# A windowed decode attention with a gated unit: Wq loaded in three transfers of 2, 6 and 24 KB per partition instead of two of 8 and 24, and x in two pieces instead of three

## The chip, the cores and the metric

The kernel runs on one core of one Trainium2 chip. The metric is device time in microseconds (us), the median of several executions. The profile is one further execution of the same program, recorded instruction by instruction and DMA packet by DMA packet.

The engines have short names: PE is TensorE (PEld its weight loads), DVE is VectorE, ACT is ScalarE, POOL is GpSimd, and SP issues transfers. SPq and ACTq are the instruction streams of SP and ACT when they issue a DMA. A core has 16 DMA engines; they are called **lanes** here, since every large transfer of this kernel is cut into 128 rows (one for each SBUF partition), eight for each lane. In the records, the transfers that SP issues are queue q1, those that ACT issues q10, and instruction fetches q8.

## What is computed

```python
xn = _layernorm(x, axis=-1)              # x: 8 x 1 x 512, bf16
# A: attention over the last W = 2048 of 8192 cached keys, 32 query heads on 8 KV heads
q = (xn @ wq)                            # wq: 512 x 4096
scores = einsum("bhqd,bhkd->bhqk", q, k) * (Dh ** -0.5)
o = einsum("bhqk,bhkd->bhqd", softmax(scores), v)
s = o @ wo                               # wo: 4096 x 512
# B: gated unit
g = _silu((_sigmoid(xn @ w_gate) * (xn @ w_up)) @ w_down)     # F = 1792
return x + s * g
```

There are 8 batch rows of one token each. The window of the K cache is 32 MB and that of the V cache 32 MB in bf16; Wq and Wo are 4 MB each, and the three weights of the gated unit 1.75 MB each. Each byte is read once, 81.01 MB in all.

## The kernel before

The order of all instructions is written out by hand; no scheduler moves them.

**Transfers.** ACT issues x (lines 124 to 129) as its first instructions, in three pieces: columns 0 to 255, 256 to 383 and 384 to 511 of the 8 rows. All the large loads go through SP by the helper `load` (its `dma_start` is line 116). SP's first two are Wq: each partition's 32 KB of Wq are 4 rows of the contraction index kt, 8 KB each, and the first transfer brings row kt = 0 (`WQ0` = 4096 elements), the second the other three. Then the K tiles (line 142, 8 tiles of 4 MB), the V tiles (line 157, 16 of 2 MB), the weights of the gated unit, and Wo in six pieces (line 185). Wq, K, the gated unit's weights and Wo share a ring of three buffers (`KRING` = 3), V has a ring of four (`VRING` = 4). `issue_loads` (line 216) issues the next load of a fixed list as soon as its ring has a buffer that the program has released; SP then waits until the buffer's last readers are done. Wq, K tile 0 and K tile 1 fill the K ring, and so K tile 2 takes the buffer of Wq and has to wait for the q projection.

**The start.** DVE computes the layernorm of x from line 244 (it waits for all pieces of x) to line 257; PE transposes xn (267) and copies x itself into another layout (272); DVE writes `xnT_sb` (285). The q projection (`q_projection`, line 396) is 32 matmuls (line 405), in the order group gg, then kt, then head gl: each reads 512 columns of row kt of Wq. `q_out` (416) casts the result on ACT (419), transposes it on DVE (424) and spreads it into `qz_sb` by copies on DVE (434) and ACT (436). `q_out` of group 0 stands before the loop, that of group 1 (line 682) after the first two K transposes.

**The loop.** From line 669 each step t transposes one eighth of a K tile on DVE (`k_turn`, line 464), multiplies q with an eighth that was transposed four steps earlier (`qk`, line 479), and, 52 steps later, multiplies the probabilities with a quarter of a V tile (`pv`, line 609). The softmax parts stand at fixed steps. At the end come the gated unit, the sum over Wo (line 723), two operations on DVE (734, 736) and the store of the result (738).

Of the kernel before, what the change touches and what calls it, by code (L numbers as in the profile page):

```python
# [10 lines left out]
def kernel(  # L11
# [16 lines left out]
    _, Hkv, Sk, Dh = A_k_cache.shape  # L28
    Hq = A_wq.shape[1] // Dh
# [3 lines left out]
    KT = D // P  # L33
# [46 lines left out]
    NSUM = 4  # L80
    NCOL = 2
    DC = D // NCOL
    WQ0 = 4096

    bf16 = mybir.dt.bfloat16
    f32 = mybir.dt.float32
# [26 lines left out]
    def load(dst, src, q=None):  # L113
        if q is None:
            q = nc.sync
        q.dma_start(out=dst, in_=src)  # L116
# [5 lines left out]
        return vring.tile(shape, bf16, name=name, tag="vring", align_bytes=ALIGN)  # L122

    x_bf = work.tile([B, D], bf16, name="x_bf")
    for c0, c1 in ((0, 2), (2, 3), (3, 4)):
        nc.scalar.dma_start(
            out=x_bf[:, P * c0 : P * c1],
            in_=A_x.flatten_outer_dims()[:, P * c0 : P * c1],
        )

    wq_sb = k_tile([P, KT, Hq * Dh], "wq_sb")
    wq_rows = A_wq.rearrange("(p kt) n -> p (kt n)", kt=KT)
    wq_flat = wq_sb[:].rearrange("p kt n -> p (kt n)")
    load(wq_flat[:, :WQ0], wq_rows[:, :WQ0])
    load(wq_flat[:, WQ0:], wq_rows[:, WQ0:])

    k_tiles = {}
    v_tiles = {}
# [633 lines left out]
```

## Time and profile before

| | before |
|---|---|
| time, median of 3 executions | 197.48 us (197.15 to 197.74) |
| the profiled execution's own time | 197.29 us |
| its span, first to last instruction | 195.5 us |
| so, around the span | 1.8 us |
| moved by q1 (all of SP's loads) | 5056 packets, 81.01 MB |
| busy: PE / DVE / ACT / POOL | 53% / 54% / 16% / 2% of the span |

The page of the profile shows the share of time in which the lanes were moving packets, in 40 slices of 4.9 us, and the rate. The *timeline* lists instructions in order of time, each with the idle time of its engine before it and what ended it. The *windows* view gives the busy time of each engine, the share of the lanes' time and the rate in any stretch; packets are counted where they begin, so a share over a short stretch can exceed 1. The *chain* goes back from the last instruction to what released each step.

The trace also keeps each DMA packet with its start, duration, size and queue. At the start of the program these records read (start of the first packet of the group, end of the last, all lanes together):

| packets | size of each | one takes | from, to (us) |
|---|---|---|---|
| first piece of x, 8 | 512 B | 25 ns | 1.71 to 1.80 |
| first transfer of Wq, 128 | 8192 B | 309 ns (the first ones up to 1044) | 1.80 to 4.99 |
| second transfer of Wq, 128 | 24576 B | 912 ns | 4.78 to 12.30 |
| second piece of x, 8 | 256 B | 18 ns | 5.70 to 5.92 |
| third piece of x, 8 | 256 B | 18 ns | 7.54 to 7.76 |
| completion packets of the third piece, 8 | 4 B | 9 ns | 8.46 to 8.67 |
| first K tile | 32768 B | 1213 ns | from 12.05 |

A transfer ends with one completion packet of 4 bytes (9 ns) on each lane that carries it; these packets raise the semaphore for which the readers wait.

### The profile page before, as it was taken

What the parts mean: (1) busy time and instruction counts of PE and PEld (TensorE: products, weight loads), DVE (VectorE), ACT (ScalarE), POOL (GpSimd) and SP (SyncE); (2) the same over time, 40 slices, a digit from 0 to 9 for tenths busy, and PEclk for the clock granted to TensorE, in tenths of its full rate; (3) what the DMA queues carried; (4) which work ended last, traced back from release to release, by engine and by line L of the source; (5) the groups of instructions that cost most, each with busy time, mean ns of one, the idle gap of its engine ahead of it and who ended that gap; (6) DMA issues with size and microseconds to landing.
All of it is one profiled execution on the core that took longest, in us unless ns stands there. A gap on an engine that the chain in (4) does not pass through costs nothing.

```text
span 195.5 us, 1888 instructions
## 1 busy us (share of the span) xinstructions
PE 102.9 (53%) x750; PEld 36.2 (19%) x750; DVE 105.5 (54%) x149; ACT 30.8 (16%) x69; POOL 4.6 (2%) x25
## 2 busy tenths in 40 slices
PE   0062014434323258403695989858944893577763
PEld 0020001101000012100121222322311131223551
DVE  0156499999899998899969726403100010040301
ACT  2025050000000084000011143511111114010100
POOL 8000000000000000000000000000000000000000
PEclk9999999999999999955588799988999798597999
DMA  7999999999999999999999999999999999999990
GB/s 276 423 476 429 436 429 429 429 429 421 429 429 429 429 429 429 389 432 463 429 419 432 436 422 429 427 429 429 429 429 432 429 431 425 431 429 432 425 390 30
DMA packets 5128, 81.14 MB, mean 415 GB/s; under 512 B 616, under 2 KB 896, under 8 KB 1152
## 3 DMA queue, kind: packets, MB, share of 16 engines
q1 hardware_dynamic: 5056, 81.01, 97.0%
q8 instruction: 6, 0.10, 0.2%
q10 hardware_dynamic: 64, 0.01, 0.0%
q14 instruction: 2, 0.02, 0.0%
HBM read 81.01 MB, written 0.01 MB: 414 GB/s over the span
## 4 chain that ended last, share of the span: by engine, by line
DMA 62%; DVE 23%; PE 10%; issue 1%; ACT 1%; SPq 0%; DVEq 0%
DMA k_sb<-in_A_k_cache_dram 31%; DMA v_sb<-in_A_v_cache_dram 22%; DVE k_sb L464 18%; DMA wo_sb<-in_A_wo_dram 10%; PE acc_ps L609 4%; DVE pt_bf L527 2%; PE s_ps L479 2%; PE pT_ps L540 2%; PE o_ps L635 2%; DVE mx L493 1%; SPq L116 0%; DVE qz_sb L434 0%; DVE o_sb L644 0%; PE den_ps L584 0%; DVE qT_sb L424 0%
## 5 line engine op out<-in xcount | busy, mean ns | idle before, releaser
L464 DVE STREAM_TRANSPOSE k_sb<-k_sb 128x1024 f32<-128x1024 f32 x64 | 73.7, 1210 | 6.7 <-DMA k_sb<-in_A_k_cache_dram 6.6
L479 PE MATMUL s_ps<-k_sb,qz_sb 128*32 128x512 bf16 x256 | 29.8, 565 | 54.2 <-DVE k_sb L464 48.4
L609 PE MATMUL acc_ps<-v_sb,pT_sb 128*64 128x512 bf16 x256 | 39.6, 443 | 10.7 <-DMA v_sb<-in_A_v_cache_dram 10.6
L644 DVE TENSOR_TENSOR o_sb<-o_ps,rden 16x512 bf16<-16x512 f32 (+2 forms) x6 | 3.0, 504 | 47.5 <-PE o_ps L635 47.5
L479 PEld LDWEIGHTS <-qz_sb 128*32 128x32 bf16 x256 | 8.5, 116 | 78.6 <-issue 55.3
L623 ACT COPY acc_sb<-acc_ps 128x512 f32<-128x512 f32 x16 | 9.4, 586 | 84.7 <-PE acc_ps L609 84.7
L609 PEld LDWEIGHTS <-pT_sb 128*64 128x64 bf16 x256 | 13.3, 120 | 31.5 <-DMA v_sb<-in_A_v_cache_dram 14.6
L635 PE MATMUL o_ps<-acc_sb,Sel 128*16 128x512 f32 (+2 forms) x48 | 15.9, 477 | 3.4 <-ACT acc_sb L623 3.4
L561 DVE TENSOR_SCALAR pT_sb<-pc_bf,Hm 128x1024 bf16<-128x1024 bf16 x16 | 6.6, 477 | 6.7 <-PE acc_ps L609 6.7
L507 ACT ACT_TABLE_LOAD x1 | 1.3, 1283 | 39.9 <-DVE nm L501 39.9
L635 PEld LDWEIGHTS o_ps<-acc_sb,Sel 128*16 128x16 f32 x48 | 4.5, 103 | 14.9 <-issue 7.7
L493 DVE TENSOR_REDUCE mx<-s_ps 128x1 f32<-128x512 f32 x8 | 5.3, 662 | 3.2 <-PE s_ps L479 3.2
L540 PE MATMUL pT_ps<-pt_bf,spread 128*128 128x512 bf16 x16 | 6.0, 501 | 1.3 <-DVE pt_bf L527 0.7
L267 PE MATMUL xnT_ps<-ident,xn_bf 8*128 8x8 bf16 x4 | 0.3, 174 | 11.6 <-DVE xn_bf L257 11.6
L436 ACT COPY qz_sb<-qT_sb 32x32 bf16<-32x32 bf16 x20 | 4.8, 241 | 8.2 <-DVE qT_sb L424 7.9
L355 PE MATMUL d_ps<-wgu_sb,xnT_sb 128*32 128x448 bf16 x32 | 3.0, 511 | 5.3 <-DMA wgu_sb<-in_B_w_up_dram 3.0
L723 PE MATMUL a_ps<-wo_sb,o_sb 128*32 128x256 bf16 x64 | 4.5, 273 | 2.0 <-DMA wo_sb<-in_A_wo_dram 2.0
L507 ACT ACTIVATE p_bf<-s_ps,nm 128x512 bf16<-128x512 f32 x8 | 5.4, 686 | 0.0
L244 DVE CAST x_f<-x_bf 8x512 f32<-8x512 bf16 x1 | 0.4, 415 | 9.2 <-DMA x_bf<-in_A_x_dram 9.2
L548 ACT CAST pc_bf<-pT_ps 128x512 bf16<-128x512 f32 x8 | 4.5, 587 | 5.0 <-DVE pt_bf L527 2.8
L527 DVE STREAM_TRANSPOSE pt_bf<-p_bf 128x512 bf16<-128x512 bf16 x8 | 4.9, 668 | 0.0
L723 PEld LDWEIGHTS <-o_sb 128*32 128x32 bf16 x64 | 3.5, 96 | 3.1 <-issue 3.0
(59 smaller groups left out, 39.4 us busy)
## 6 DMA issues: line engine op xcount, KB each, us to landing
k_sb<-in_A_k_cache_dram SPq DMA_DIRECT2D x8, 4096.0 KB, 19.3
v_sb<-in_A_v_cache_dram SPq DMA_DIRECT2D x16, 2048.0 KB, 15.7
wq_sb<-in_A_wq_dram SPq DMA_DIRECT2D x1, 3072.0 KB, 11.4
wo_sb<-in_A_wo_dram SPq DMA_DIRECT2D x1, 2048.0 KB
wgu_sb<-in_B_w_gate_dram SPq DMA_DIRECT2D x1, 1792.0 KB
wgu_sb<-in_B_w_up_dram SPq DMA_DIRECT2D x1, 1792.0 KB, 24.7
wd_sb<-in_B_w_down_dram SPq DMA_DIRECT2D x1, 1792.0 KB
wq_sb<-in_A_wq_dram SPq DMA_DIRECT2D x1, 1024.0 KB, 4.6
```

Source lines behind the costliest of these rows:

```text
L436: nc.scalar.copy(out=out, in_=in_)
L464: nc.vector.transpose(out=kw, in_=kw)
L479: nc.tensor.matmul(s_tiles[i][32 * g : 32 * (g + 1), :], lhsT=qz_sb[:, hb, h, 2 * a + e, :], rhs=kT[:, :, a, h, :, e], start=(n == 0), sto ...
L493: nc.vector.reduce_max(out=mx_of[hb][:, kq : kq + 1], in_=s_tiles[i][:], axis=AX.X)
L507: nc.scalar.activation(out=p_bf[:, :, kq], in_=s_tiles.pop(NK * hb + kq)[:].rearrange("p (o c j) -> p c j o", o=2, j=NC), func=AF.Exp, bia ...
L527: nc.vector.transpose(out=pt[:, w * n : w * (n + 1)], in_=p_bf[:, w * n : w * (n + 1)])
L540: nc.tensor.matmul(pT_ps[:], lhsT=spread[:, gg, y].rearrange("p k g -> p (k g)"), rhs=pt[:, c, y, :], start=(y == 0), stop=(y == 1), skip_ ...
L561: nc.vector.tensor_scalar(out=pT_of[hb, gg][:, :, gl, :], in0=pc, scalar1=Hm[:, gl : gl + 1], scalar2=None, op0=ALU.mult,)
L609: nc.tensor.matmul(acc_tiles[i][w * c : w * (c + 1), :], lhsT=pT[:, GL * rep * ch : GL * rep * ch + w], rhs=v_tiles[i][:, ch : ch + NCH, : ...
L623: nc.scalar.copy(out=acc_sbs[i // NSUM][:, i % NSUM], in_=acc_tiles.pop(i)[:])
L635: nc.tensor.matmul(o_ps[rows, :n, :], lhsT=Sel[:, c].rearrange("p g r -> p (g r)"), rhs=acc_sb[:, :, Dh * c : Dh * (c + 1)], start=(c == 0 ...
L723: nc.tensor.matmul(a_ps[32 * c : 32 * (c + 1), :], lhsT=o2_sb[:, k, :], rhs=wo_parts[k][:, DC * c : DC * (c + 1)], start=(k == 0), stop=(k ...
```

## The change

The split of Wq becomes a list of bounds, in elements of each partition's 16384: 0, 1024, 4096, 16384. The first 8 KB, one transfer before, come in 2 KB and 6 KB; the last 24 KB stay one transfer. The second and third piece of x become one. SP issues one DMA more and ACT one less; the number of DMAs stays the same, and so do the semaphores that later transfers take in turn. In the order of instructions, PE's third matmul of the q projection (heads gl = 2, 3 of kt = 0) has a new wait, for the second transfer of Wq; the fifth (kt = 1) waits for the last transfer, as before. PE's copy of x waits for two pieces instead of three. Nothing else moves on any engine.

```diff
-    WQ0 = 4096
+    WQ_AT = (0, 1024, 4096, KT * Hq * Dh)
...
-    for c0, c1 in ((0, 2), (2, 3), (3, 4)):
+    for c0, c1 in ((0, 2), (2, 4)):
         nc.scalar.dma_start(
             out=x_bf[:, P * c0 : P * c1],
             in_=A_x.flatten_outer_dims()[:, P * c0 : P * c1],
...
-    load(wq_flat[:, :WQ0], wq_rows[:, :WQ0])
-    load(wq_flat[:, WQ0:], wq_rows[:, WQ0:])
+    for n0, n1 in zip(WQ_AT, WQ_AT[1:]):
+        load(wq_flat[:, n0:n1], wq_rows[:, n0:n1])
```

## The prediction

> **What bounds the kernel now.** I read the DMA rows of the page first. Here are the lanes' busy share in tenths and the rate, in 40 slices:
>
> ```profile
> DMA  7999999999999999999999999999999999999990
> GB/s 276 423 476 429 436 429 429 429 429 421 429 429 429 429 429 429 389 432 463 429 419 432 436 422 429 427 429 429 429 429 432 429 431 425 431 429 432 425 390 30
> ```
>
> Between the first and the last slice the lanes never rest. The windows view says it more finely (us; busy time of PE, PEld, DVE, ACT, POOL with counts; PE's clock; lanes' share; GB/s):
>
> ```profile
> 0.00:1.80 1.80, 0.00 (x0) 0.00 (x0) 0.00 (x0) 0.00 (x0) 1.20 (x7) 1.00 0.01 2
> 1.80:5.00 3.20, 0.00 (x0) 0.00 (x0) 0.00 (x0) 1.28 (x1) 3.03 (x17) 1.00 1.19 451
> 5.00:22.35 17.35, 4.24 (x38) 1.49 (x38) 6.28 (x24) 3.76 (x12) 0.36 (x3) 1.00 1.00 431
> 22.35:60.00 37.65, 13.28 (x112) 4.18 (x113) 36.83 (x38) 2.89 (x12) 0.00 (x0) 1.00 1.00 431
> ...
> 140.00:180.00 40.00, 24.98 (x166) 9.55 (x164) 2.99 (x5) 5.93 (x9) 0.00 (x0) 0.85 1.01 430
> 180.00:190.30 10.30, 7.48 (x94) 5.25 (x92) 1.99 (x3) 0.96 (x2) 0.00 (x0) 0.92 0.99 414
> 190.30:192.11 1.81, 1.59 (x22) 0.89 (x17) 0.00 (x0) 0.00 (x0) 0.00 (x0) 1.00 0.33 115
> 192.11:195.50 3.39, 0.29 (x2) 0.09 (x1) 0.70 (x2) 0.00 (x0) 0.00 (x0) 0.96 0.01 2
> ```
>
> From 1.80 to 190.3 us the share is 0.99 to 1.01 at 430 GB/s; DVE, nearly as full from 22 to 60 us (36.83 of 37.65), holds the lanes up nowhere. To see how close it comes, I set the bytes that SP had issued against the bytes moved, at each of SP's later issues: the least that was still queued is 2.56 MB, 6.2 us of work at 431 GB/s, at the K tile issued at 64.64 us. A load could be issued 6 us later and no lane would notice. So the time is a sum: start of the stream (1.80) + its length (to 192.11) + a tail of 3.40 (two matmuls, two DVE operations, the store) = 195.51, and 1.78 around the span makes 197.29, which is 0.19 below the median of the runs, 197.48.
>
> The timeline of the start shows why the work on x and q doesn't count (start, duration, what, [idle before <- what ended it]):
>
> ```profile
> 0.74 1.27 ACTq L126 DMA_DIRECT2D x_bf<-in_A_x_dram  x3
> ...
> 0.74 0.89 SPq L116 DMA_DIRECT2D wq_sb<-in_A_wq_dram  x2
> ...
> 9.15 0.41 DVE L244 CAST x_f<-x_bf 8x512 f32<-8x512 bf16 x1 [9.15 <-DMA x_bf<-in_A_x_dram]
> ...
> 12.19 3.69 PE L405 MATMUL q_ps<-wq_sb,xnT_sb 128*32 128x512 bf16 x32
> ...
> 17.89 0.48 DVE L652 MEMSET o_sb<- 128x512 uint32 x1
> 22.35 2.37 DVE L464 STREAM_TRANSPOSE k_sb<-k_sb 128x1024 f32<-128x1024 f32 x2 [3.98 <-DMA k_sb<-in_A_k_cache_dram]
> ```
>
> x lands at 9.15, the q projection ends at 15.88, DVE is through with everything it can do at 18.37, and then it sits 3.98 us until K tile 0 lands. The chain of waits agrees: it passes from SP's issues straight into the landing of that tile, by no instruction of x or q:
>
> ```profile
> 1.22 0.41 SPq L116
> 1.63 0.05 issue
> 1.68 20.65 DMA k_sb<-in_A_k_cache_dram
> ```
>
> **The change part by part.** *The split of Wq, as packets.* Each lane carried 8 packets of 8192 B at 309 ns. Now it carries 8 of 2048 B, which the pieces of Wo and others show at 84 ns, and 8 of 6144 B. That size is not in the trace; 4096 B take 159 ns and 8192 B 309, and the middle is 234. So 84 + 234 - 309 = 9 ns for each row, 8 rows: 72 ns, and one more completion packet, 9 ns. Sum: **+0.08 us** of stream on every lane.
>
> *x in two pieces.* The eight lanes that carry x spend 25 + 18 + 18 ns on data and three times 9 on completions now, and 2 x 25 + 2 x 9 afterwards: -0.02 us on those, nothing on the other eight. The stream ends with its slowest lane, so +0.06 to +0.08; I take **+0.07**.
>
> *The extra issue on SP.* One issue takes 0.41 to 0.64 us (Wq 0.42 and 0.41, K tile 0 0.64). K tiles 0 and 1 are issued some 0.46 us later, at 2.14 instead of 1.68; 4 MB are queued then, 9.7 us of work. Without that queue it would cost the 0.46.
>
> *The hand-over from the first to the second transfer* is the one place where the lanes could run dry. SP's first issue starts at 0.74 and its first packet at 1.80, 1.06 later. The second issue starts at 1.22, so its packets are there at 2.28. The first transfer keeps a lane busy for 8 x 84 = 0.67 us from 1.80, to 2.47 at the earliest. In truth it lasts longer, since the first packets are slow: over their row's 309 ns the first ones took up to 735 ns more, 0.41 us on average over the lanes. That leaves 0.2 to 0.6 us of margin: cost 0. From there the 6 KB packets last 1.87 us, and the third issue, at about 1.68, is there by 2.74.
>
> *The slow first packets themselves* are the term that the trace does not show for 2 KB. Bounds: if small first packets do away with that loss, -0.41; if they pay it twice, once for each size, +0.41. I take 0: it looks like the time to the first data, common to any size, and the nearest row is the same queue's own first packets.
>
> *x earlier.* The second piece of x is issued at 1.37, and 0.97 us after its issue the first piece was moving; so it was ready near 2.3, about when the second transfer of Wq was, and it came to its turn only behind eight 8 KB packets and one of 24 KB, at 5.70. Then data and completions of q10 alternated with single packets of 24 KB, 0.91 us each, until 8.67. With 2 KB packets ahead and 6 KB packets in between, the same order gives x at about 1.80 + 0.4 + 0.67 + 2 x 0.234 + the 0.5 that DVE starts after the last completion = 3.8; if all eight 6 KB packets and two of 24 KB go ahead first, 7.2. Either way 2 to 5 us before 9.15. DVE's part, PE's transposes and POOL's constants (done at 5.4) move ahead; but the q projection must wait at its fifth matmul for the last 24 KB of Wq. That landed 11.4 us after its issue at 1.22, at 12.6, and now 0.08 later. Its 28 matmuls at 0.107 follow: 15.7 instead of 15.88. So 5 us on x shrink to 0.2 on q, and these go into DVE's 3.98 us of waiting. The new wait on PE (third matmul, second transfer) has only q matmuls behind it; should q come late, DVE's 3.98 us and, for the issue of K tile 2 at 15.92, a queue of 15.9 us are in front of any harm.
>
> *ACT's missing issue*, 0.325 us, brings the table load forward to about 1.7; ACT then waits for DVE at 10.53 anyway: 0.
>
> *Tail.* Nothing there is touched: 0.
>
> **Sum:** 197.29 + 0.07 = 197.36 for a profiled execution; by the median, 197.48 + 0.07 = **197.55 us**. That is 0.04%, and a measurement of this kernel tells about 0.3% (0.6 us) from no change.
>
> **Rivals.** *Slower: a transfer pays its start each time.* If the second transfer began only when the first was through, as the first began 1.06 us after its issue, the lanes would stand idle for up to 1.06 us: 198.6. It decides as soon as packets of the second transfer reach the lanes after the first's have run out (2.5 to 2.9 us). Against it: the second transfer of Wq moves its first packet at 4.78 while the first's last ends at 4.99, and at the end Wo's pieces of 256 and 128 KB follow each other without a gap, 46 ns a packet. For it: those had time in the queue, and these have 0.2 to 0.6 us.
> A rule of the Trainium skill stands behind this rival. Its page "DMA: Bandwidth & Descriptors", "Rules for kernel authors", wants 1 MiB and more per DMA and small transfers merged; here 1 MB becomes 256 and 768 KB. "Anatomy of one DMA", for transfers issued by GpSimd, fits a fixed 2.0 us per DMA; as an estimate by that page, one more DMA in the stream is 199.5. The rows above speak against it wherever a transfer is queued behind another.
>
> *Faster: the start of q was on the path.* If DVE's first transposes hung on q and not on K tile 0, 2 us from x would come off: 195.5. The 3.98 us of idle time that a K landing ends, and a stream that never rests, speak against it. A smaller gain is possible at the tail: at 190.3 us most lanes are done, and a few, which instruction fetches had delayed by about 1 us each, run until 191.8 (share 0.33 above). Should a fetch fall elsewhere, up to 1 us goes: 196.5. PE's instructions, the bulk of the program, stay the same, so I don't expect it.
>
> *The change doesn't do what it says:* x's second piece still waits behind packets of 24 KB and lands near 8 to 9 us. The time is the same, 197.5, for the same reason as in the forecast.
>
> **How the numbers follow.** Forecast 0.69, x not earlier 0.11 (same time), a start paid again 0.12, faster (q on the path 0.03, lanes at the tail 0.05) 0.08. So within 0.3%: 0.80, slower 0.12, faster 0.08. Range: 197.55 - 0.41 - 0.1 = 197.0 and 197.55 + 0.41 + 0.1 = 198.1, with 0.1 for the scatter of a median of runs that lie 0.6 apart; most of both rivals stay outside.
>
> **What would show it.** In the profile after: lanes at 1.00 from about 2.5 on, no dip at the hand-over; 128 packets more; K tile 0 landing within 0.4 us of 22.35; DVE starting on x between 3.8 and 7.2, the q projection ending near 15.7, DVE's wait before line 464 still about 4 us. Wrong would be: idle lanes between 2.3 and 3.5 us, Wo's end more than 0.5 us away from 192.1, or DVE released at 22 us by something other than a K landing.

## The result and the profile after

| | before | after |
|---|---|---|
| time, median | 197.35 us (19 runs, 197.03 to 197.82) | 197.75 us (19 runs, 197.51 to 198.19) |
| ratio | | 1.0019, 95% interval 1.0011 to 1.0026 |
| profiled execution: time, span | 197.29, 195.5 us | 197.56, 195.6 us |

The change makes the kernel about 0.37 us longer (0.2 to 0.5). That is within the 0.3% that the prediction called the same, and inside its range; but it is measurable, and five times the 0.07 of the sum. One run of the kernel before, at 253.11 us, stands far from all the others and is left out of every mean and ratio below.

The DMA rows of the page after, in the same 40 slices:

```profile
DMA  6999999999999999999999999999999999999990
GB/s 220 448 439 429 429 442 435 442 442 434 429 442 429 429 429 429 395 429 459 429 405 429 432 425 432 434 435 432 425 432 429 432 425 435 433 424 432 420 386 31
```

The lanes are as full as before from the second slice on. Only the first slice differs: 220 GB/s where 276 stood. The timeline of the start shows what became of x and q:

```profile
4.41 0.43 DVE L244 CAST x_f<-x_bf 8x512 f32<-8x512 bf16 x1 [4.41 <-DMA x_bf<-in_A_x_dram]
...
7.46 0.62 PE L405 MATMUL q_ps<-wq_sb,xnT_sb 128*32 128x512 bf16 x4
...
13.02 3.18 PE L405 MATMUL q_ps<-wq_sb,xnT_sb 128*32 128x512 bf16 x28 [4.94 <-DMA wq_sb<-in_A_wq_dram]
...
18.20 0.48 DVE L652 MEMSET o_sb<- 128x512 uint32 x1
22.68 2.37 DVE L464 STREAM_TRANSPOSE k_sb<-k_sb 128x1024 f32<-128x1024 f32 x2 [3.99 <-DMA k_sb<-in_A_k_cache_dram]
```

x is on DVE at 4.41 instead of 9.15, and four q matmuls run at 7.46. The other 28 then wait 4.94 us for the last 24 KB of Wq, and the projection ends at 16.20, later than the 15.88 of before. DVE waits 3.99 us for K tile 0, as long as ever, but the tile lands 0.33 us later. So all that was gained on x is lost in waiting, and the tile's delay must come from the stream itself. The windows view around the first transfers (PE, PEld, DVE, ACT, POOL, clock, lanes' share, GB/s; packets count where they begin) says where. Before the change:

```profile
1.70:2.30 0.60, 0.00 (x0) 0.00 (x0) 0.00 (x0) 0.26 (x1) 0.60 (x2) 1.00 1.13 225
2.30:2.90 0.60, 0.00 (x0) 0.00 (x0) 0.00 (x0) 0.60 (x1) 0.54 (x4) 1.00 0.63 232
2.90:4.00 1.10, 0.00 (x0) 0.00 (x0) 0.00 (x0) 0.42 (x1) 1.10 (x8) 1.00 1.08 454
```

And after it:

```profile
1.70:2.30 0.60, 0.00 (x0) 0.00 (x0) 0.00 (x0) 0.60 (x1) 0.60 (x2) 1.00 0.68 159
2.30:2.90 0.60, 0.00 (x0) 0.00 (x0) 0.00 (x0) 0.60 (x1) 0.54 (x4) 1.00 1.38 410
2.90:4.00 1.10, 0.00 (x0) 0.00 (x0) 0.00 (x0) 0.06 (x1) 1.10 (x8) 1.00 0.83 287
```

Before, the stream has its slow start once, and from 2.9 us it is at its full rate (454 GB/s in the view, some 430 in the long run). After, the rate is only 287 between 2.9 and 4.0, when the second transfer, the 6 KB rows, has taken over. The 410 ahead of it proves less: slow packets of 6 KB that begin in that window are counted there whole.

For the experiments I need a number for this. The packet records give each packet's duration; what a packet takes beyond the steady duration of its size (84 ns for 2 KB, 234 for 6 KB, 309 for 8 KB, and so on), summed over a transfer and divided by 16, is its **excess** per lane. Before: 0.41 us in the first transfer, 0.01 in the second. After: 0.19 in the first, 0.31 in the second, 0.01 in the third. The second transfer pays a start of its own. It isn't that every packet was slow at that time: of the packets that begin between 2.6 and 2.9 us, 10 of the 13 of 6 KB take over 3% longer than their steady duration, and none of the 32 of 2 KB does. Nor were the lanes empty: between 2.9 and 4.0 us each stood idle for only 0.06 us on average. The packets were there, and took longer.

### The profile page after: what moved, and what is told of

Its sections match the earlier page's. It is cut to its first block, busy times and chain, and to the rows that moved or that the text cites. A ratio compares the mean times of both kernels' runs of the same rounds, so it can differ in the third digit from the quotient of the medians.

```text
span 195.6 us, 1889 instructions
## 1 busy us (share of the span) xinstructions
PE 102.8 (53%) x750; PEld 37.2 (19%) x750; DVE 105.5 (54%) x149; ACT 31.0 (16%) x69; POOL 4.8 (2%) x25
## 4 chain that ended last, share of the span: by engine, by line
DMA 64%; DVE 22%; PE 10%; SPq 1%; issue 1%; DVEq 0%
DMA k_sb<-in_A_k_cache_dram 31%; DVE k_sb L464 18%; DMA v_sb<-in_A_v_cache_dram 17%; DMA wo_sb<-in_A_wo_dram 16%; PE acc_ps L609 4%; PE a_ps L723 3%; PE s_ps L479 2%; PE pT_ps L540 1%; DVE pt_bf L527 1%; SPq L116 1%; DVE mx L493 1%; DVE qz_sb L434 0%; DVE qT_sb L424 0%; DVE prod L734 0%; DVE y_bf L736 0%
## 5 line engine op out<-in xcount | busy, mean ns | idle before, releaser
L609 PE MATMUL acc_ps<-v_sb,pT_sb 128*64 128x512 bf16 x256 | 37.2, 421 | 10.8 <-DMA v_sb<-in_A_v_cache_dram 10.8
L609 PEld LDWEIGHTS <-pT_sb 128*64 128x64 bf16 x256 | 12.7, 116 | 30.7 <-DMA v_sb<-in_A_v_cache_dram 15.2
L635 PE MATMUL o_ps<-acc_sb,Sel 128*16 128x512 f32 (+2 forms) x48 | 16.5, 494 | 3.4 <-ACT acc_sb L623 3.4
L723 PE MATMUL a_ps<-wo_sb,o_sb 128*32 128x256 bf16 x64 | 5.3, 346 | 2.9 <-DMA wo_sb<-in_A_wo_dram 2.9
L405 PE MATMUL q_ps<-wq_sb,xnT_sb 128*32 128x512 bf16 x32 | 3.8, 626 | 4.9 <-DMA wq_sb<-in_A_wq_dram 4.9
L723 PEld LDWEIGHTS <-o_sb 128*32 128x32 bf16 x64 | 4.6, 122 | 3.7 <-issue 3.1
L424 DVE STREAM_TRANSPOSE qT_sb<-q_sb 128x512 bf16<-128x512 bf16 x2 | 1.4, 689 | 6.7 <-ACT q_sb L419 6.7
```

The lines of the kernel that those rows point to most:

```text
L609: nc.tensor.matmul(acc_tiles[i][w * c : w * (c + 1), :], lhsT=pT[:, GL * rep * ch : GL * rep * ch + w], rhs=v_tiles[i][:, ch : ch + NCH, : ...
L635: nc.tensor.matmul(o_ps[rows, :n, :], lhsT=Sel[:, c].rearrange("p g r -> p (g r)"), rhs=acc_sb[:, :, Dh * c : Dh * (c + 1)], start=(c == 0 ...
L723: nc.tensor.matmul(a_ps[32 * c : 32 * (c + 1), :], lhsT=o2_sb[:, k, :], rhs=wo_parts[k][:, DC * c : DC * (c + 1)], start=(k == 0), stop=(k ...
```

## The experiments

Three theories stood at the outset. H: the second transfer's packets come when the first's run out, without data read ahead. X: x's second piece, moving in the middle of the small packets, disturbs them. P: only the added packets cost anything. S, C and L are rivals of H that came up on the way; each expectation says what it means.

**The split alone.** x stays in three pieces:

```diff
-    for c0, c1 in ((0, 2), (2, 4)):
+    for c0, c1 in ((0, 2), (2, 3), (3, 4)):
```

> Wq in 2, 6 and 24 KB, x still in three pieces. Measured so far: the change made the kernel 1.0019 times as long (+0.37 us), and K tile 0, on which DVE starts line 464, landed 0.33 us later (22.68 against 22.35). Theory H (hand-over): the packets of the second Wq transfer reach the lanes when the first, only 16 KB per lane, is nearly through, so that they start without data read ahead; the whole loss belongs to the split. Then line 464 starts at 22.65 to 22.75 and the time is +0.3 to +0.45 us. Theory X (x): the loss comes from x's second piece, which now moves in the middle of the 6 KB packets (3.1 to 4.0 us); with x in three pieces there are two such interruptions, and the loss grows to 0.5 us or more (22.85). Theory P (packets alone): only the 8 packets and one completion more per lane cost anything, 0.08 us: 22.43, time +0.08.

Measured: ratio 1.0026 (1.0015 to 1.0037), +0.51 us; line 464 at 22.91; excess 0.13 and 0.34. The loss belongs to the split; P is out. The size is what X said rather than H, but the interval overlaps that of the change, so it is not shown that x's third piece costs anything.

**x alone**, with Wq in 8 and 24 KB:

```diff
-    WQ_AT = (0, 1024, 4096, KT * Hq * Dh)
+    WQ_AT = (0, 4096, KT * Hq * Dh)
```

> Wq in 8 and 24 KB as before, x in two pieces. H and P: no loss, two completions and one row less on the lanes of x: line 464 starts at 22.30 to 22.36, time within 0.1 us of before; x is on DVE near 7.2 instead of 9.15, since one turn behind 24 KB packets for data and one for completions (1.8 us) fall away. X: x's second piece moves at 5.70 beside 24 KB packets, as it did before; no loss either. If the time is more than 0.2 us longer, none of the three is right.

Measured: 1.0002 (0.9993 to 1.0011), line 464 at 22.45, x on DVE at 7.27, excess 0.47 and 0.00. Two pieces for x cost nothing and bring x 1.9 us forward, for nothing. Line 464 is a little outside what was expected, with the same head as before: a first sign of the scatter between executions.

**A longer first transfer**, 4, 4 and 24 KB: `WQ_AT = (0, 2048, 4096, KT * Hq * Dh)`.

> Wq in 4, 4 and 24 KB, x in two pieces: as many packets and transfers as in the change, but the first transfer keeps a lane busy for 8 x 0.159 = 1.27 us instead of 0.67, so the second one's packets, there at about 2.28, come well before the first's run out (3.1 at the earliest). H: most of the loss goes; line 464 starts at 22.40 to 22.48, time +0.05 to +0.15 us. A rival S (small packets are slow in a cold stream, wherever they stand): 4 KB rows in both of the first transfers lose nearly as much as 2 and 6 KB; 22.6 to 22.7, time +0.3.

Measured: 1.0013 (1.0004 to 1.0022), +0.26 us; line 464 at 22.57. Both numbers lie between H and S. The packets tell the two parts apart: excess 0.55 in the first transfer and 0.00 in the second. With 1.27 us of work ahead of it the second transfer pays no start, as H has it. And most of x's second piece moved between 3.9 and 4.4 us among 4 KB packets, which took not a nanosecond longer: X falls. Half of the 0.26 us does not lie in the stream at all, as the table below shows.

**The same first transfer with no third**, 2 and 30 KB: `WQ_AT = (0, 1024, KT * Hq * Dh)`.

> Wq in two transfers of 2 and 30 KB, x in two pieces: 16 packets per lane as before the change, and as many transfers, so packets and completions cost nothing (84 + 1138 ns a row against 309 + 912). H: the hand-over after 16 KB per lane is the same as in the change; line 464 starts at 22.5 to 22.65, time +0.15 to +0.3 us. P: 22.35, time the same. S: only the 2 KB rows are slow, 0.19 us of loss in the changed kernel's packets against 0.41 in the first 8 KB rows of before: 22.15 to 22.35, time -0.2 to 0.

Measured: 1.0010 (1.0001 to 1.0018), +0.20 us; line 464 at 22.66, just past H's range; excess 0.18 and 0.29. With the packet count of before, the second transfer pays its start again, as H has it; P and S said no loss.

**A shorter first transfer**, 1, 7 and 24 KB: `WQ_AT = (0, 512, 4096, KT * Hq * Dh)`.

> Wq in 1, 7 and 24 KB, x in two pieces. So far: in the changed kernel the first 6 KB packets of the lanes take 0.3 us longer than later ones (summed over a lane), the first 2 KB packets 0.19; with 4, 4 and 24 KB the second transfer's packets have no such excess, and with 2 and 30 KB they have it again, 0.29. Theory H (the second transfer's packets come when the first runs out, and pay a start of their own): here the first transfer lasts only 8 x 0.046 = 0.37 us a lane from 1.80, so it runs out before the second is there (2.28). The excess and the idle time after 2.2 us grow: line 464 starts at 22.75 to 23.1, time +0.4 to +0.7 us against before. A rival C (every transfer costs the same, whenever it comes; the change is +0.2 to +0.4 for one transfer more): 22.6 to 22.75, time +0.37 like the change.

Measured: 1.0026 (1.0016 to 1.0036), +0.51 us; line 464 at 22.83; excess 0.09 and 0.57. The second transfer's excess grows as the first gets shorter: 0.00 behind 4 KB rows, 0.31 and 0.20 behind 2 KB, 0.57 behind 1 KB. C, by which every transfer costs the same, doesn't give that, though the time alone (0.32 to 0.71 us) would not rule it out.

**Three transfers with the long one first**, 8, 6 and 18 KB: `WQ_AT = (0, 4096, 7168, KT * Hq * Dh)`.

> Wq in 8, 6 and 18 KB, x in two pieces: three transfers and 24 packets a lane, as in the change, but the first lasts 2.4 us a lane, so that the second and third are queued long before they are needed. H: only packets and completion remain, +0.08 us: line 464 at 22.38 to 22.52, time 0 to +0.15 us. C: like the change, 22.6 to 22.75 and +0.37. x is on DVE near 6 us.

Measured: 1.0009 (0.9999 to 1.0018), +0.18 us; excess 0.42, 0.05 and 0.02. The same 6 KB rows, queued in time, pay 0.05 instead of 0.31 or 0.20. Line 464 started at 22.65, later than H said. The packet records explain part of it: the lanes end K tile 0 at 22.01 on average, 0.12 us later than before the change (21.83, 21.92 and, with x in two pieces alone, 21.91), and that is the added packets and the 0.05. The rest is the last lane, for which the tile waits: it ends 0.29 us behind that average, against 0.15 to 0.29 in the three others. What sets this spread is open.

**The second transfer in time, by the other queue.** The 6 KB transfer becomes ACT's first issue; x's loop moves behind Wq's (not shown):

```diff
-    for n0, n1 in zip(WQ_AT, WQ_AT[1:]):
-        load(wq_flat[:, n0:n1], wq_rows[:, n0:n1])
+    for n, (n0, n1) in enumerate(zip(WQ_AT, WQ_AT[1:])):
+        load(wq_flat[:, n0:n1], wq_rows[:, n0:n1], nc.scalar if n == 1 else None)
```

> Wq in 2, 6 and 24 KB as in the change, but the 6 KB transfer is ACT's first issue (at 0.74, ahead of x), so that its packets are there at about 1.8 with the 2 KB packets and alternate with them; SP issues the 24 KB transfer second, at 1.2. The same bytes, packets and transfers. H: no hand-over any more; the excess of the first packets is one start (0.4 to 0.5 us a lane, as before the change), line 464 at 22.38 to 22.5, time +0.05 to +0.2 us. C: as the change, 22.68 and +0.37. x comes later than in the change, which no theory counts.

Measured: 1.0005 (0.9996 to 1.0014), +0.10 us; excess 0.33 and 0.12, one start's worth between them; line 464 at 22.62, later than expected. Same bytes, same packets, same number of transfers as the change, and most of its cost is gone. About half of what is gone, 0.13 us, is time around the span (1.81 against 1.94 us in the table below); the other 0.10 is in the stream.

**x far too late.** The kernel before, with x's three issues moved from ACT to SP, behind Wq (the move isn't shown):

```diff
-        nc.scalar.dma_start(
+        nc.sync.dma_start(
             out=x_bf[:, P * c0 : P * c1],
```

> The kernel before, but x's three pieces are issued by SP behind the two transfers of Wq instead of by ACT ahead: x lands with the end of Wq, so DVE begins on x at 12.7 to 13.2 instead of 9.15, and the q projection ends near 19.5 instead of 15.88. If the start of q isn't on the path (forecast), this 3.6 us goes into DVE's 3.98 us of waiting: line 464 at 22.3 to 22.5, time within 0.15 us of before. If q's start is on the path, +3 us or more.

Measured: 1.0019 (1.0010 to 1.0029), +0.37 us, more than I expected. x came to DVE at 13.64, beyond the 13.2 that I expected and 4.5 us later than before, and used up DVE's wait to the last bit: line 464 starts at 22.80 with no idle time before it.

```profile
22.80 2.37 DVE L464 STREAM_TRANSPOSE k_sb<-k_sb 128x1024 f32<-128x1024 f32 x2
```

No bracket stands behind this line: DVE itself was late, not the K tile. That would cost several us if q's start were on the path, and it costs tenths. Where these come from, the second profile and the table below tell.

**One transfer for Wq**, to which H pointed: `WQ_AT = (0, KT * Hq * Dh)`.

> Wq in one transfer of 32 KB a partition, x in two pieces: the version to which the other runs point, without any hand-over and with 8 packets and one completion less per lane than before the change (1213 ns a row against 309 + 912). Theory H: the stream starts like before (0.4 to 0.5 us of excess in the first packets) and is 0.07 us shorter; line 464 at 22.25 to 22.4, time -0.15 to +0.05 us against before, so between nothing and a gain too small for this measurement. A rival L (a longer first packet costs more at the cold start): the first packets' excess grows with their size (0.19 for 2 KB, 0.41 for 8 KB rows), 0.6 to 0.8 us here; 22.5 to 22.8, +0.1 to +0.4 us. x waits behind packets of 1.21 us and is on DVE near 7.5.

Measured: 1.0016 (1.0007 to 1.0025), +0.32 us; line 464 at 22.63; excess 0.70. All three lie where L put them, and H was incomplete: the first packets take up to 2.26 us where later ones of the same size take 1.21, a larger loss than any shorter first row had.

Over the first transfers of SP the excess reads 0.09 (1 KB), 0.13 to 0.25 (2 KB; 0.33 where ACT's 6 KB rows start beside them), 0.55 (4 KB), 0.39 to 0.48 (8 KB), 0.70 (32 KB). For 1, 4 and 32 KB this is one profile each. So neither fewer nor more transfers than 8 and 24 KB were faster than the kernel before; no version here beats it.

**Repeats**, to see what scatters:

> The kernel before, profiled once more, to see how much of the head repeats: all theories expect the first 8 KB packets to lose 0.35 to 0.5 us a lane again, and line 464 between 22.30 and 22.45. If it comes at 22.6 or later, the difference in the head that the theories explain is scatter between executions.

> The changed kernel, profiled once more. Theory H: the first 6 KB packets of the lanes again take 0.25 to 0.35 us a lane longer than later ones, the first 2 KB packets 0.15 to 0.25, line 464 at 22.6 to 22.75. If the 6 KB packets' excess is gone, H falls.

> The kernel with x behind Wq on SP, profiled once more. In its first profile DVE started line 464 at 22.80 by its own lateness (0.45 us after the K tile's landing), the stream was level with before until 60 us, and then packets took some per cent longer between 65 and 120 us, 0.5 us in all, with no lane idle. If that stretch is scatter, it is elsewhere or gone here; if it belongs to DVE's later place, it is at 65 to 120 us again.

Before, again: line 464 at 22.52, a little beyond the expected 22.45, excess 0.39 and 0.00.

```profile
22.52 2.37 DVE L464 STREAM_TRANSPOSE k_sb<-k_sb 128x1024 f32<-128x1024 f32 x2 [3.98 <-DMA k_sb<-in_A_k_cache_dram]
```

After, again: 22.73, excess 0.25 and 0.20; the second is smaller than H expected, and not gone.

```profile
22.73 2.37 DVE L464 STREAM_TRANSPOSE k_sb<-k_sb 128x1024 f32<-128x1024 f32 x2 [4.00 <-DMA k_sb<-in_A_k_cache_dram]
```

The rates repeat less well. Before, again:

```profile
2.30:2.90 0.60, 0.00 (x0) 0.00 (x0) 0.00 (x0) 0.60 (x1) 0.54 (x4) 1.00 0.65 246
2.90:4.00 1.10, 0.00 (x0) 0.00 (x0) 0.00 (x0) 0.42 (x1) 1.10 (x8) 1.00 1.02 432
```

And after, again:

```profile
2.30:2.90 0.60, 0.00 (x0) 0.00 (x0) 0.00 (x0) 0.60 (x1) 0.54 (x4) 1.00 1.06 342
2.90:4.00 1.10, 0.00 (x0) 0.00 (x0) 0.00 (x0) 0.07 (x1) 1.10 (x8) 1.00 0.96 359
```

The rate of after is again lower than before's between 2.9 and 4.0 us (359 against 432 GB/s), but it does not fall there, it rises from 342.

So the start of line 464 scatters by 0.2 between executions, and the difference, 22.35, 22.52 and (x alone) 22.45 against 22.68 and 22.73, is about 0.27. The late x, again: line 464 at 22.71, again without a wait, and the slower packets between 65 and 120 us are gone; the span is 195.4, no longer than before. That stretch was scatter. The second profile of after has one of its own (20 to 85 us, 0.4 us), and before's first has a short one at 45 to 55 (0.16 us). So in the first pair of profiles K tile 0 lands 0.33 us later, and the last packets of Wo only 0.06.

**The table over all of them.** The runs give the span beside the time, so I could split each kernel's mean time into span and what lies around it. The fourth column is the mean, over the 16 lanes, of the end of each lane's last packet of K tile 0:

| Wq, KB (x on ACT) | transfers before K by SP | excess, us | lanes end K tile 0, mean | line 464 at | mean span (against before, same session) | around it |
|---|---|---|---|---|---|---|
| 8, 24 (before) | 2 | 0.41, 0.01; 0.39, 0.00 | 21.83; 21.92 | 22.35; 22.52 | 195.50 to 195.58 | 1.79 to 1.82 |
| 8, 24, x in two | 2 | 0.47, 0.00 | 21.91 | 22.45 | 195.62 (+0.04) | 1.81 |
| 2, 6, 24 (after) | 3 | 0.19, 0.31; 0.25, 0.20 | 22.09; 22.01 | 22.68; 22.73 | 195.80 (about +0.23) | 1.94 |
| 2, 6, 24, x in three | 3 | 0.13, 0.34 | 22.18 | 22.91 | 195.97 (+0.39) | 1.93 |
| 4, 4, 24 | 3 | 0.55, 0.00 | 22.01 | 22.57 | 195.69 (+0.11) | 1.93 |
| 1, 7, 24 | 3 | 0.09, 0.57 | 22.15 | 22.83 | 195.89 (+0.39) | 1.94 |
| 8, 6, 18 | 3 | 0.42, 0.05 | 22.01 | 22.65 | 195.60 (+0.10) | 1.94 |
| 2, 24 (6 by ACT) | 2 | 0.33, 0.12 | 21.97 | 22.62 | 195.63 (+0.13) | 1.81 |
| 2, 30 | 2 | 0.18, 0.29 | 22.02 | 22.66 | 195.74 (+0.16) | 1.83 |
| 32 | 1 | 0.70 | 22.01 | 22.63 | 195.79 (+0.28) | 1.85 |
| 8, 24, x by SP | 5 | 0.44, 0.02; 0.48, 0.00 | 21.83; 21.93 | DVE late | 195.63 (+0.14) | 2.07 |

Each mean is over 7 to 34 runs, and a difference against before is uncertain by 0.1 to 0.2 us. The span of before isn't on record for the session of after; +0.23 is the difference of the mean times, 0.37, less the 0.14 around the span. Two things stand in the table. By and large the span follows the landing of K tile 0: the later line 464, the longer the span (8, 6 and 18 KB is the exception). And the time around the span, which I had taken as one number, is 1.79 to 1.83 with two transfers of SP ahead of K, 1.93 or 1.94 in all five kernels with three, and 2.07 with five. It does not fall with one (1.85). Most of what the kernel with the late x loses, 0.27 us, lies there.

## Why the prediction was right, and what it missed

The time came out nearly the same for the reason that the prediction gave: the stream sets it, and x and q end in a wait. The size did not come from the sum, and that it stayed inside the range was in part luck: the 0.41 us either way was put there for the first packets, and covered two other misses. The sum's parts, one by one:

- *The stream sets the time* held. The lanes are full from the second slice on, K tile 0 lands straight out of the queue, and DVE's wait of 3.99 us is there as forecast. With x 1.9 us earlier (two pieces alone) the mean span is 0.04 us longer than before, with x 4.5 us later 0.14: the start of q moves it by little more than a tenth, and neither difference is clear of noise. One reading was too smooth: the share of 0.99 to 1.01 at 430 GB/s does not hold from 1.80 us on, where the prediction's own row has 1.19 and 451 up to 5.00, nor at the end, where it has 414.
- *x* came at 4.41, inside 3.8 to 7.2, nearest to the order in which packets of both queues alternate (the terms behind the 7.2 add up to 7.1). The rival that x would not overtake is out. *The q projection* ended at 16.20, not near 15.7: the last 24 KB of Wq came with the delayed stream, and PE went on at 13.02 rather than 12.7; its 28 matmuls took 3.18 us, 0.114 each instead of 0.107.
- *Packets and completions*, 0.08 less 0.02: the 6 KB rows take 234 ns as interpolated, queue q1 moves 5200 packets instead of 5056 (the 128 foretold and 16 completions), and nothing speaks against the term.
- *The hand-over* was forecast at **0**, with 0.2 to 0.6 us of margin. That step failed. I compared the arrival of the second transfer with the end of the first, and took a packet that is there in time for a packet at full speed. It was there in time: the first of 6 KB begins at 2.61 us, when the first lanes are through with the first transfer. But such packets took up to 836 ns instead of 234. What they waited for no record shows. The prediction had named a dip and idle lanes as the sign of this mistake; the low rate is there (287 and 359 GB/s against 454 and 432), the idle lanes hardly. The rows pay 0.2 to 0.3 us, and nothing when the 1.27 us of the 4 KB rows lie ahead.
- *The slow first packets* were held equal, bounded by 0.41 either way. They fell, from about 0.4 to 0.2. Together the starts of first and second transfer come to 0.45 to 0.50 against 0.39 to 0.47, so the two errors nearly cancel in the mean over the lanes. The lanes end K tile 0 some 0.16 us later on average (22.09 and 22.01 against 21.83, 21.92 and 21.91), of which the added packets are 0.07. The K tile, which needs the slowest lane, lands 0.27 later in the mean of the profiles.
- *Around the span* I had carried 1.78 over unchanged. It grew by 0.14 (1.94 against 1.80). No step of the prediction looked there.

So the loss reads: about 0.14 around the span, and about 0.23 in it; on the mean of the profiles all of the second part is present when K tile 0 lands. Of the 0.23 the added packets explain 0.06 to 0.08. The rest goes with the hand-over in the experiments. Where the second transfer is queued in time (4, 4 and 24 KB; 8, 6 and 18; by ACT), the mean span is 0.10 to 0.13 above before's, little more than the packets; with 2 and 30 KB, which add no packet, it is 0.16, and with 1, 7 and 24 KB 0.39. No single one of these stands clear of its neighbour; together with the packet records they point one way. What the hand-over takes on which lane isn't settled, since single profiles scatter by 0.2.

The slower rival, *a transfer pays its start each time*, named the right place and a start that is paid again, but as idle lanes and with too high a price: the lanes were hardly idle, and the slow packets cost 0.2 to 0.3 us instead of 1.06. The Trainium skill ("DMA: Bandwidth & Descriptors", "Rules for kernel authors") would merge small transfers. The sign agrees with the change. The size, 0.37 us, is far from the 2.0 us per DMA that the prediction took as an estimate from the fit in "Anatomy of one DMA", which is for transfers issued by GpSimd. And merging both transfers of Wq into one was slower than before by 0.32, which the rule does not say. Of the faster rivals nothing showed: the lanes delayed by instruction fetches were there as before, the last Wo packets ending at 191.88 against 191.82.

## What to carry to other kernels

Where a full DMA queue sets the time, speeding up what is fed by it first gains nothing; look for what ends the wait of the first big consumer, here the K tile. A transfer that should follow another without a loss has to be queued well before the other ends, and splitting the very first transfer takes that time away. By the prediction's estimate the second transfer is there at 2.28 us; the first lanes were through with the first at 2.6 behind 2 KB rows, 0.3 us later, which was too little, and at 3.5 behind 4 KB rows, 1.2 us later, which was enough. And a sum over the span should not carry the time around the span as a constant when an edit changes the number of issues.

## What the runs showed of the hardware beyond that

- The loss at the start of the stream differed with the size of the rows that start it: 0.1 us a lane for 1 KB, 0.13 to 0.25 for 2 KB, 0.4 to 0.55 for 4 and 8 KB, 0.7 for 32 KB. Where the first transfer lost little, the second lost the more: both together make 0.45 to 0.66 us behind 1 and 2 KB rows.
- The time around the span grew with the number of transfers that SP issued, 1.80, 1.94 and 2.07 us for two, three and five ahead of K, while x's number of pieces on ACT did not move it (1.81). No trace shows that time, so its cause is open.
- In some executions packets take a few per cent longer for tens of us with no lane idle (0.2 to 0.6 us in all), at a place that changes from one execution to the next.
